# A recurrent attention and a two-layer network on one core: loads moved to GpSimd's queue, and more operands turned by transposing DMAs

## The chip, the cores and the metric

The kernel runs on one core of one Trainium2 chip. The metric is the device time of one execution in microseconds (us). The core has five engines with a queue of instructions each: TensorE (PE, matrix products), VectorE (DVE), ScalarE (ACT), GpSimd (POOL) and SyncE (SP). SP and POOL also issue DMAs, which sixteen DMA engines carry out. Each queue is worked off in order: an instruction that waits holds all that stand behind it.

## The reference

The first part is a gated linear attention over 4 batches, 8 heads, 768 steps and 48 channels per head:

```python
for t in range(S):
    state = alpha[:, :, t, :, None] * state + np.einsum('bhd,bhe->bhde', k[:, :, t], v[:, :, t])
    y[:, :, t] = np.einsum('bhd,bhde->bhe', q[:, :, t], state)
```

The second part takes the 3072 rows of 384 values (all heads of one step side by side) through two matrices:

```python
h = x @ w_in                 # 384 -> 2048
r = np.maximum(h, 0.0)
out = (r * r) @ w_out        # 2048 -> 384
```

## The kernel before

**Chunks.** The 4 x 768 steps are cut into 24 chunks of 128 steps, numbered s = 0 to 23; six chunks are one batch (`c` counts 0 to 5 in it, `last` is c = 5, which needs no state after it). Within a chunk the recurrence is turned into matrix products. With L the logarithm of alpha and P its running sum over the steps of the chunk, q is multiplied by exp(P) and k by exp(-P). The products of these two, cut off above the diagonal, are the scores (`sc`, then `sm`); scores times v, plus scaled q times the state of the chunks before, is the output of the chunk (`py`, copied to `xn`). The state (`st`) adds scaled k times v and is then scaled by exp of the chunk's total.

**Two ways to the scaled q and k.** The scores need q and k with the channels on the partitions, the state product needs k with the steps on them.

- In early chunks (s below `RAW`, 11) the running sum with the steps on the partitions (`e_p0`, one 128x384 product, and four one-column products for the totals) goes through two exponentials (`A`, `Ainv`), DVE makes scaled q and k (`qA_s` L502, `kI_s` L505), and TensorE transposes both (`e_p1q`, `e_p1k`), four products each.
- In later chunks ("raw") POOL casts q and k to bf16 (`rawb`, L413), SP's transposing DMAs turn them (`rawt`, L416), TensorE makes the running sum already turned (`e_pT`, four products), ACT takes its two exponentials (L451 and L454), and DVE multiplies (L507 `e_qAT`, L510 `e_kiT`). Unless the chunk is the last of its batch, `e_p0`, `Ainv` and `kI_s` are still made as before, for the state product alone.

**From attention to the network.** `xn` is turned to `xT_big` by three transposes on TensorE and a copy on DVE; from chunk 18 to 22 (`XTURN`) by one transposing DMA from SP (L620). The first matrix then works in groups of two chunks (products `bank<-xT_big,w_in_b`, relu on ACT L676, square on DVE L684 into `gT`), the second on one chunk at a time (`bank<-w_out_b,gT`, copied to `ob` by ACT or DVE). Outputs leave from SP, those of chunks 5 to 17 that are not held back from POOL (L772).

**Order.** A planner in the kernel (`Plan.run`) gives each step an engine, a reckoned duration, what it depends on and a priority, lists the steps in time with these figures, and emits the instructions in the order of their reckoned starts. The order on each engine is thus fixed before the run: attention steps of chunk s stand between matrix products of chunks some 3.7 earlier (`LEAD`). The planner's classes are PE, ACT, DVE and POOL, "DMA" for loads (first in, first out, 1.0 us each), "TR" for transposing DMAs (1.0 us, landing 4.0 us later) and "OUT"; the last three all go to SP's queue. POOL does casts of v (L405), of raw q and k, and the outputs named above.

**Loads.** Each chunk has four loads of 128 x 8 x 48 fp32 (192 KB, in pieces of 48 values): alpha, q, k and v (`add_load`, L371). All are issued by SP, between its transposes; alpha of chunks 0 to 3 comes as two larger loads. There are six buffers for each of the four.

Of the kernel before, what the change touches and what calls it, by code (L numbers as in the profile page):

```python
# [54 lines left out]
def after(op, x=0.0):  # L55
    return (op, x)
# [85 lines left out]
def kernel(  # L142
# [10 lines left out]
    nc = tc.nc  # L153
# [4 lines left out]
    NP = H // 2  # L158
# [35 lines left out]
        out=utri_f, in_=utri_f, compare_op=ALU.is_ge, fill=0.0,  # L194
# [10 lines left out]
    for c in range(JN):  # L205
        blk = slice(JP * c, JP * c + JP)
        nc.gpsimd.affine_select(
            out=tri4[blk, 0:JW], in_=tri4[blk, 0:JW], compare_op=ALU.is_ge, fill=0.0,
# [27 lines left out]
    def pin(ins):  # L236
        tc.keep_in_program_order(ins)
# [4 lines left out]
    def tr(*a):  # L242
        pin(nc.tensor.transpose(*a))  # L243
# [6 lines left out]
    GLA_BANKS = sl_bank[0:2]  # L250
# [14 lines left out]
    def add(eng, dur, emit, *deps, **kw):  # L265
        return plan.add(Op(eng, dur, emit, deps, **kw))
# [41 lines left out]
    C = [dict() for _ in range(NT)]  # L308
    state = {}
    SRC = dict(srcs)  # L310
    EARLY = 4
    RAW = 11
    XTURN = (18, 23)
    TLD, TLAT, TLATE = 1.0, 4.0, 2.0
    NR = 3
    R = {}

    def raw_tiles():
        if R:
            return  # L320
        R["b"] = stage.tile([P, NR, 2, H, DP], BF16, name="rawb", tag="stage")
        nc.gpsimd.memset(R["b"][:, :, :, :, D:], 0.0)
        R["t"] = stage.tile([P, NR, 2, NP, P], BF16, name="rawt", tag="stage")
        R["i"] = stage.tile([P, 2, NP, P], BF16, name="aiT", tag="stage")

# [38 lines left out]
    def add_load(s, nm):  # L364
        d = C[s]
        b, c = divmod(s, NCH)

        def ld():
            if nm not in d:
                d[nm] = loads.tile([P, H, D], FP32, name=nm)  # L370
            pin(nc.sync.dma_start(out=d[nm], in_=SRC[nm][b, c]))  # L371
        prev = C[s - LB].get("use_" + nm) if s >= LB else None
        d["ld_" + nm] = add("DMA", LD if s < 4 else LD1, ld, prev, lat=2.0 if s < 4 else LAG if s < 6 else 2.4, at=0.6)

    def add_chunk(s):
        d = C[s]
        b, c = divmod(s, NCH)
        i = s % NBUF
        L, qA, kI, ae = L_s[:, i], qA_s[:, i], kI_s[:, i], ae_s[:, i]
        old = C[s - NBUF].get("end") if s >= NBUF else None  # L380
        g = dict(prio=-10.0 + s * 0.01)
        last = c == NCH - 1

        def cast(op, out_t, in_t):
            if op.eng == "ACT":
                pin(nc.scalar.copy(out_t, in_t))  # L386
            elif op.eng == "DVE":
                pin(nc.vector.tensor_copy(out_t, in_t))  # L388
            else:
                pin(nc.gpsimd.tensor_copy(out_t, in_t))  # L390
# [6 lines left out]
        if joint:  # L397
            ln = J["ln"]
        else:
            ln = [add("ACT", 0.41, e_ln, d["ld_at"], old, prio=-15.0 if s < EARLY else -5.0)]  # L400
# [5 lines left out]

        raw = s >= RAW
        if raw:
            w, wz = s % NR, s % 2

            def e_rb(j, nm):
                raw_tiles()
                pin(nc.gpsimd.tensor_copy(R["b"][:, w, j, :, 0:D], d[nm]))  # L413

            def e_turn(j):
                pin(nc.sync.dma_start_transpose(out=R["t"][:, w, j], in_=R["b"][:, w, j].rearrange("p h d -> p (h d)")))  # L416
            rt = []
            for j, nm in enumerate(["qt", "kt"]):
                cb = add("POOL", 0.55, lambda j=j, nm=nm: e_rb(j, nm), d["ld_" + nm],
                         *([C[s - NR]["turn"][j]] if s >= RAW + NR else []), prio=-5.0)  # L420
                d["use_" + nm] = cb
                t_ = add("TR", TLD, lambda j=j: e_turn(j), cb, *([C[s - NR]["turned"][j]] if s >= RAW + NR else []), lat=TLAT)
                t_.late = TLATE
# [17 lines left out]
        p0 = Op("PE", 0.66 if joint else 0.17 if raw else 0.27, e_p0, ln, takes=GLA_BANKS, lat=0.05, **g)  # L441
# [14 lines left out]
        def e_aeT(j):  # L456
            rows = slice(64 * j, 64 * j + 64)
            pin(nc.scalar.activation(ae[rows, :, j], d["pmT"][rows, :, P - 1], AF.Exp))
# [11 lines left out]

        def e_ae1():
            pin(nc.scalar.activation(ae[64:128, :, 1], d["pm"][64:128, HD:HD + NP], AF.Exp))
        if not (raw and last):
            plan.add(p0)
        if not raw:
            a_ = add("ACT", 0.38, e_A, p0, **g)
            ai = add("ACT", 0.38, e_Ai, p0, after(a_), **g)
        if raw:
            ai = None
            if not last:  # L480
                ai = add("ACT", 0.38, e_Ai, p0, **g)
                p0.gives = ai
            pT = Op("PE", 0.23, e_pT, [*ln] + ([] if last else [after(p0)]), takes=GLA_BANKS, **g)
            plan.add(pT)
            if last:
                pT.gla = s
            aT = add("ACT", 0.48, e_AT, pT, after(ai) if ai else None, **g)
            aiT = add("ACT", 0.48, e_AiT, pT, after(aT), *([C[s - 2]["turned"][1]] if s >= RAW + 2 else []), **g)
            pT.gives = aiT
            if not last:  # L490
                ae0 = add("ACT", 0.18, lambda: e_aeT(0), pT, after(aiT), **g)
                pT.gives = ae1 = add("ACT", 0.19, lambda: e_aeT(1), pT, after(ae0), **g)
        elif joint:
            ae1 = J["ae"]
            p0.gives = ai
        else:
            ae0 = add("ACT", 0.18, e_ae0, p0, after(ai), **g)
            ae1 = add("ACT", 0.19, e_ae1, p0, after(ae0), **g)
            p0.gives = ae1
# [8 lines left out]

        def e_kiT():
            pin(nc.vector.tensor_mul(d["qkT"][:, NP:2 * NP, :], R["t"][:, w, 1], R["i"][:, wz]))  # L510
        if raw:
            if not last:
                mk = d["use_kt"] = add("DVE", 0.47, e_kI, ai, d["ld_kt"], old, **g)
            cp = add("DVE", 0.34, e_qAT, aT, rt[0], **g)
            cpk = add("DVE", 0.34, e_kiT, aiT, rt[1], cp, **g)
            d["turned"] = [cp, cpk]
        else:
            mq = d["use_qt"] = add("DVE", 0.47, e_qA, a_, d["ld_qt"], old, **g)
            mk = d["use_kt"] = add("DVE", 0.47, e_kI, ai, d["ld_kt"], old, **g)
# [11 lines left out]
        if not raw:  # L531
            p1q = plan.add(Op("PE", 0.22, e_p1q, [mq], takes=GLA_BANKS, **g))
            p1k = plan.add(Op("PE", 0.22, e_p1k, [mk] if s < EARLY else [mk, after(p1q)], lat=0.15,
                              takes=P1K_BANKS if s < EARLY else None, **g))

        def e_cp(lo, hi):
            if "qkT" not in d:
                d["qkT"] = work.tile([P, 2 * NP, P], BF16, name="qkT")
            cast(cpk if lo else cp, d["qkT"][:, lo:hi, :], d["pTk"][:, 0:NP, :] if lo else d["pT"][:, lo:hi, :])
        if s < EARLY:  # L540
            cp = add({"ACT": 0.49, "DVE": 0.34}, 0, lambda: e_cp(0, NP), p1q, **g)
            cpk = add({"DVE": 0.34, "ACT": 0.49}, 0, lambda: e_cp(NP, 2 * NP), p1k, **g)
# [13 lines left out]
        p2 = d["p2"] = plan.add(Op("PE", 0.42, e_p2, [cp, cpk], takes=[sl_sc], lat=0.10, **g))  # L556
# [9 lines left out]
        if not last:  # L566
# [7 lines left out]
            prev = C[s - 1].get("sb") if s else None  # L574
            if c == 0 and s:
                prev = C[s - 2]["sb"]
# [37 lines left out]
        def e_p4():  # L614
            d["px"] = psum(p4, [P, KT, P], BF16)
            for j in range(KT):
                tr(d["px"][:, j, :], d["xn"][:, j * P:(j + 1) * P], ident_bf)
        if XTURN[0] <= s < XTURN[1]:
            def e_xt():
                pin(nc.sync.dma_start_transpose(out=xT_big[:, :, s * P:(s + 1) * P], in_=d["xn"]))  # L620
# [238 lines left out]
    for op in plan.order:  # L859
        if op.eng == "PE":  # L860
# [3 lines left out]
            if pe_end is not None and DUMMY and not opened and op.start < CALM:  # L864
                n = max(0, int((op.start - pe_end) / 0.11 + (0.4 if op.start < DENSE else -1.8))) + (extra.pop(0) if extra else 0)
# [35 lines left out]
```

## Time and profile before

| | |
|---|---|
| median of 3 runs | 185.1 us (184.77 to 185.87) |
| profiled execution | 185.07 us, of it span 183.4 us |
| instructions | 4946 |
| TensorE: matmuls, busy | 1908, 177.5 us |
| DVE, ACT, POOL busy | 127.1, 126.5, 39.4 us |
| granted clock | 1.00 |
| DMA | 34.12 MB, 80.7% of 16 engines' span on SP's queue, 3.2% on POOL's |

The span is the time from the first to the last instruction of the core; what the whole execution takes beyond it lies around the kernel. In a line of a timeline the columns are start, length in us, engine, source line, operation, destination and sources with their sizes, count, and in brackets the idle time before with what ended it. A line with "<-" in a list of waits reads: this engine, at this line, stood idle for that one, with total, count and longest in us. In the lines of stretches each engine has its busy time and the number of instructions (PE, PEld, DVE, ACT, POOL), then the granted clock, the mean share of the DMA engines that was busy, and GB/s. Matmuls overlap in the records: each shows some 200 to 330 ns, while the next starts earlier.

### The profile page before, as it was taken

To read this page: it belongs to the slowest core of one execution; us is meant where nothing else is said; L and a number is where in the kernel's file an instruction comes from. 1 tells how busy PE (TensorE), PEld (TensorE's weight loads), DVE (VectorE), ACT (ScalarE), POOL (GpSimd) and SP (SyncE) were. 2 spreads that over 40 slices of the span, in tenths; PEclk is the share of its full clock that TensorE was granted. 3 is DMA by queue.
4 is the path that set the end of the run, shared out by engine and by line. 5 is a ranking of instruction groups with operands and counts; after the bars stand their busy time and mean duration, and the time that the engine had idled before them with its cause. 6 is when DMAs were issued, how large, how long until landed. Compare 5 with 4: busy or idle time off the path is not lost.

```text
span 183.4 us, 4946 instructions
## 1 busy us (share of the span) xinstructions
PE 177.5 (97%) x1908; PEld 130.5 (71%) x1908; DVE 127.1 (69%) x273; ACT 126.5 (69%) x286; POOL 39.4 (21%) x80
## 2 busy tenths in 40 slices
PE   7999999899999999999999998999999999999993
PEld 2577884567769877867768776667766777778663
DVE  1179898684999998778877867748855984744200
ACT  3677799226859996966967859847975895767321
POOL 8221100021131142132223133342323512000000
PEclk9999999999999999999999999999999999999999
DMA  5999999999999999998999599898898898901022
GB/s 168 215 212 252 302 366 321 326 220 204 177 191 201 194 179 173 141 190 161 150 193 202 113 240 186 161 227 162 170 201 182 176 163 194 301 13 43 12 77 86
DMA packets 120200, 34.12 MB, mean 186 GB/s; under 512 B 112400, under 2 KB 118928, under 8 KB 120176
## 3 DMA queue, kind: packets, MB, share of 16 engines
q1 hardware_dynamic: 119536, 31.83, 80.7%
q0 software_dynamic: 640, 1.97, 3.2%
q8 instruction: 15, 0.25, 0.6%
q14 instruction: 9, 0.07, 0.2%
HBM read 25.17 MB, written 4.72 MB: 163 GB/s over the span
## 4 chain that ended last, share of the span: by engine, by line
PE 49%; DMA 2%; ACT 1%; issue 0%; DVE 0%
PE bank L240 45%; DMA at<-in_alpha_dram 2%; PE sc L240 2%; PE st L240 1%; PE bank L243 1%; ACT aiT L454 0%; ACT r L676 0%; ACT ob L758 0%; ACT L_s L396 0%; ACT ob L716 0%; DVE xT_big L388 0%; ACT qkT L451 0%
## 5 line engine op out<-in xcount | busy, mean ns | idle before, releaser
L240 PE MATMUL bank<-xT_big,w_in_b 128*128 128x256 bf16 (+2 forms) x636 | 76.6, 262 | 0.9 <-ACT r L676 0.7
L240 PE MATMUL bank<-w_out_b,gT 128*128 128x384 bf16 (+1 forms) x400 | 71.6, 320 | 0.5 <-DVE w_out_b L296 0.5
L676 ACT ACTIVATE r<-bank 128x512 bf16<-128x512 f32 x96 | 56.6, 606 | 11.3 <-PE bank L240 9.9
L240 PEld LDWEIGHTS <-w_in_b 128*128 128x128 bf16 x636 | 52.7, 98 | 10.6 <-issue 1.5
L240 PEld LDWEIGHTS <-gT 128*128 128x128 bf16 x416 | 37.2, 98 | 18.7 <-DVE w_out_b L296 1.0
L684 DVE TENSOR_TENSOR gT<-r 128x512 bf16<-128x512 bf16 x96 | 41.8, 453 | 10.2 <-ACT r L676 9.0
L561 DVE TENSOR_TENSOR sm<-sc,utri_b 128x512 bf16<-128x512 f32 x48 | 30.8, 684 | 5.9 <-PE sc L240 5.7
L405 POOL CAST vb<-vt 128x384 bf16<-128x384 f32 x24 | 13.6, 569 | 69.1 <-DMA vt<-in_v_dram 55.2
L386 ACT CAST xn<-bank 128x384 bf16<-128x384 f32 x24 | 11.6, 482 | 11.6 <-PE bank L240 11.5
L505 DVE TENSOR_TENSOR kI_s<-kt,Ainv 128x384 bf16<-128x384 f32 x21 | 12.8, 611 | 7.8 <-ACT Ainv L466 7.8
L240 PEld LDWEIGHTS <-qkT 64*128 64x128 bf16 (+1 forms) x272 | 10.7, 95 | 6.4 <-issue 2.4
L586 ACT CAST sb<-st 128x384 bf16<-128x384 f32 x20 | 9.6, 482 | 7.7 <-DVE st L581 7.5
L758 ACT COPY ob<-bank 128x384 f32<-128x384 f32 x14 | 6.7, 480 | 8.0 <-PE bank L240 8.0
L396 ACT ACTIVATE L_s<-at 128x384 bf16<-128x384 f32 x20 | 10.5, 527 | 2.4 <-DMA at<-in_alpha_dram 2.3
L240 PE MATMUL bank<-warm 128*128 128x256 bf16 (+1 forms) x54 | 10.9, 348 | 1.3 <-DVE warm L188 1.3
L502 DVE TENSOR_TENSOR qA_s<-qt,A 128x384 bf16<-128x384 f32 x11 | 6.3, 575 | 8.0 <-ACT A L462 8.0
L413 POOL CAST rawb<-qt 128x384 bf16<-128x384 f32 x13 | 7.4, 570 | 20.3 <-DMA qt<-in_q_dram 20.3
L413 POOL CAST rawb<-kt 128x384 bf16<-128x384 f32 x13 | 7.6, 587 | 19.0 <-DMA kt<-in_k_dram 11.1
L581 DVE TENSOR_TENSOR st<-st,ae_s 128x384 f32<-128x384 f32 x20 | 11.1, 556 | 0.5 <-PE st L240 0.5
L466 ACT ACTIVATE Ainv<-bank 128x384 bf16<-128x384 f32 x21 | 10.5, 501 | 1.1 <-PE bank L240 1.0
L240 PE MATMUL sc<-qkT 64*128 64x128 bf16 x192 | 9.5, 219 | 0.0
L240 PEld LDWEIGHTS <-sm 128*128 128x128 bf16 x192 | 8.1, 96 | 1.7 <-issue 0.2
(64 smaller groups left out, 165.7 us busy)
## 6 DMA issues: line engine op xcount, KB each, us to landing
qt<-in_q_dram SPq DMA_DIRECT2D x24, 192.0 KB, 4.0
kt<-in_k_dram SPq DMA_DIRECT2D x24, 192.0 KB, 3.6
vt<-in_v_dram SPq DMA_DIRECT2D x24, 192.0 KB, 3.8
at<-in_alpha_dram SPq DMA_DIRECT2D x20, 192.0 KB, 4.0
wo<-in_moe_w_out_dram SPq DMA_DIRECT2D x4, 768.0 KB, 8.5
out_dram<-ob POOLq DMA_DIRECT2D x10, 192.0 KB, 3.1
wi<-in_moe_w_in_dram SPq DMA_DIRECT2D x4, 384.0 KB, 5.3
wi<-in_moe_w_in_dram SPq DMA_DIRECT2D x2, 768.0 KB, 8.3
```

Source lines behind the costliest of these rows:

```text
L240: pin(nc.tensor.matmul(*a, **kw))
L386: pin(nc.scalar.copy(out_t, in_t))
L396: pin(nc.scalar.activation(L[:, :, 0:D], d["at"], AF.Ln))
L405: pin(nc.gpsimd.tensor_copy(d["vb"], d["vt"]))
L413: pin(nc.gpsimd.tensor_copy(R["b"][:, w, j, :, 0:D], d[nm]))
L466: pin(nc.scalar.activation(d["Ai"], d["pm"][:, 0:HD].rearrange("p (h d) -> p h d", h=H), AF.Exp, scale=-1.0))
L505: pin(nc.vector.tensor_mul(kI[:, :, 0:D], d["kt"], d["Ai"]))
L561: pin(nc.vector.tensor_mul(d["sm"][:, hh], d["sc"][:, hh], utri_b.to_broadcast([P, NP, P])))
L581: pin(nc.vector.tensor_mul(st4, st4, bcast(ae, D)))
L586: pin(nc.scalar.copy(d["sbt"], d["st"]))
L676: pin(nc.scalar.activation(box["r"][:, 0:w], box["ph"][:, 0:w], AF.Relu))
L684: pin(nc.vector.tensor_mul(gT[g][:, f0:f0 + per, lo * P:lo * P + n], r, r))
```

## The change

Four things change:

- Loads of chunk 12 and later (`PL`) are issued by POOL. In the planner such a load is a step of POOL of 0.9 us that lands 5.0 us later (`PL_LAT`) and may not start before the scores of the chunk three earlier (`PL_AHEAD`); this condition only orders the steps, the instruction itself waits for its buffer.
- `RAW` is 10 in place of 11: chunk 10 takes the later way to its scaled q and k.
- `XTURN` begins with chunk 16 in place of 18: x of chunks 16 and 17 is turned by DMA too.
- From chunk 18 on (`KTURN`), unless the chunk is the last of its batch (18 to 22), `e_p0`, `Ainv` and the DVE product for `kI_s` are left out. Scaled k, which DVE has already made with the channels on the partitions for the scores, is turned back into `kI_s` by a transposing DMA from SP (`e_kn`), and the state product waits for that.

Together there are 48 loads from POOL in place of SP, and nine transposing DMAs more (two for chunk 10, two of x, five of keys). The core of the diff:

```diff
-    RAW = 11
-    XTURN = (18, 23)
+    RAW = 10
+    PL, PL_AHEAD, PL_LAT = 12, 3, 5.0
+    XTURN = (16, 23)
...
+    KTURN = 18
...
-            pin(nc.sync.dma_start(out=d[nm], in_=SRC[nm][b, c]))
+            pin((nc.gpsimd if s >= PL else nc.sync).dma_start(out=d[nm], in_=SRC[nm][b, c]))
         prev = C[s - LB].get("use_" + nm) if s >= LB else None
+        if s >= PL:
+            o = d["ld_" + nm] = add("POOL", 0.9, ld, prev, C[s - PL_AHEAD]["p2"], prio=4.0, lat=PL_LAT)
+            o.moves = 0.85
+            return
...
+        kd = s >= KTURN and not last
+        nat = not (s >= RAW and (last or kd))
...
-        if not (raw and last):
+        if nat:
             plan.add(p0)
...
-            if not last:
+            if nat:
                 ai = add("ACT", 0.38, e_Ai, p0, **g)
                 p0.gives = ai
...
+        def e_kn():
+            pin(nc.sync.dma_start_transpose(out=kI.rearrange("p (n a) d -> p n (a d)", a=2),
+                                            in_=d["qkT"][:, NP:2 * NP, :].rearrange("p n t -> p (n t)")))
         if raw:
-            if not last:
+            if nat:
                 mk = d["use_kt"] = add("DVE", 0.47, e_kI, ai, d["ld_kt"], old, **g)
             cp = add("DVE", 0.34, e_qAT, aT, rt[0], **g)
             cpk = add("DVE", 0.34, e_kiT, aiT, rt[1], cp, **g)
             d["turned"] = [cp, cpk]
+            if kd:
+                mk = add("TR", 0.65, e_kn, cpk, old, lat=TLAT)
+                mk.late = 0.5
```

More of the change, by code (lines that the diff above doesn't have):

```diff
@@ L479, in add_chunk @@
             ai = None
-            if not last:
+            if nat:
                 ai = add("ACT", 0.38, e_Ai, p0, **g)
                 p0.gives = ai
-            pT = Op("PE", 0.23, e_pT, [*ln] + ([] if last else [after(p0)]), takes=GLA_BANKS, **g)
+            pT = Op("PE", 0.23, e_pT, [*ln] + ([after(p0)] if nat else []), takes=GLA_BANKS, **g)
             plan.add(pT)
-            if last:
+            if not nat:
                 pT.gla = s
```

## The prediction

> **What bounds the kernel now.** I read the busy shares first, then the stretches of the middle of the run, then TensorE's own timeline, and last what the few gaps wait for. TensorE is busy for 97% of the span, no other engine for more than 71%.
>
> ```profile
> PE 177.5 (97%) x1908; PEld 130.5 (71%) x1908; DVE 127.1 (69%) x273; ACT 126.5 (69%) x286; POOL 39.4 (21%) x80
> ...
> rawt<-rawb SPq DMA_TRANSPOSE x26, 3.4
> ```
>
> In stretches of 20 us from 60 to 160 us, which is where the change acts, TensorE idles 0.75 of 100 us at full clock. DVE and ACT each have 23 us to spare, POOL 71. The DMA engines do not: their shares add up to 93 of 100 us.
>
> ```profile
> 60.00:80.00 20.00, 20.00 (x244) 16.19 (x241) 18.31 (x39) 16.60 (x39) 5.48 (x10) 1.00 0.96 174
> 80.00:100.00 20.00, 19.92 (x210) 14.79 (x209) 15.54 (x34) 14.98 (x35) 5.90 (x11) 1.00 1.00 176
> 100.00:120.00 20.00, 19.33 (x197) 14.24 (x196) 14.48 (x34) 15.84 (x37) 5.80 (x11) 1.00 0.90 180
> 120.00:140.00 20.00, 20.00 (x202) 14.09 (x199) 13.44 (x28) 14.52 (x35) 7.28 (x14) 1.00 0.91 189
> 140.00:160.00 20.00, 20.00 (x212) 15.18 (x211) 14.52 (x30) 14.75 (x34) 4.38 (x8) 1.00 0.88 200
> ```
>
> So a matrix instruction less is time less, as long as nothing new makes TensorE wait. Matmuls overlap in the records, so their price is the distance from one start to the next. The timeline of TensorE has the pairs:
>
> ```profile
> 66.38 0.24 PE L240 MATMUL bank<-ones_t,L_s 128*128 128x1 bf16 x4
> 66.48 0.36 PE L240 MATMUL bank<-vb,sm 128*128 128x48 bf16 x8
> ...
> 68.31 0.33 PE L243 MATMUL bank<-ident_bf,xn 128*128 128x128 bf16 x3
> 68.48 1.46 PE L240 MATMUL bank<-w_out_b,gT 128*128 128x384 bf16 x8
> ...
> 69.83 0.38 PE L243 MATMUL bank<-ident_bf,qA_s 128*128 128x128 bf16 x4
> 70.05 0.49 PE L240 MATMUL bank<-xT_big,w_in_b 128*128 128x256 bf16 x3
> ...
> 73.34 0.39 PE L240 MATMUL bank<-utri_b,L_s 128*128 128x128 bf16 x4
> 73.56 0.49 PE L240 MATMUL bank<-xT_big,w_in_b 128*128 128x256 bf16 x3
> ...
> 128.17 0.33 PE L240 MATMUL bank<-L_s,utri_b 128*128 128x384 bf16 x1
> 128.33 0.49 PE L240 MATMUL bank<-xT_big,w_in_b 128*128 128x256 bf16 x3
> ```
>
> The one gap of the middle is 0.66 us before 111.84. The chain of waits leads it back to an alpha load on SP's queue, and the list of waits names it:
>
> ```profile
> 105.28 4.13 DMA at<-in_alpha_dram
> 109.42 0.34 ACT L_s L396
> ...
> 110.70 0.60 ACT aiT L454
> ```
>
> ```profile
> PE bank L240 <- ACT r L676: 0.7, 1, 0.7
> ```
>
> ACT stood 0.71 us behind a logarithm whose load was late, and the relu behind it kept TensorE. On SP that load stood behind a transpose that held the queue for 3.48 us.
>
> **The change, part by part.** As built, the changed program has 19 matmuls less. *Cumulative sum of chunks 18 to 22* (128x384, the line at 128.17): 5 x 0.16 = 0.80 us off. *Transposes of x of chunks 16 and 17* (68.31 to 68.48): 2 x 0.17 = 0.34 off. *Chunk 10 turned by DMA*: q and k lose four transposes each (0.22 + 0.22) and the four one-column products (0.10), and it gains four transposed sums (73.34 to 73.56, 0.22): 0.32 off. Together 1.46 us off the engine that sets the end.
>
> What goes with it on DVE and ACT (five Ainv at 0.50 us, five kI at 0.61, two x copies at 0.35, chunk 10's exponentials and products swapped) I cost at nothing: the matrix work covers it, with 23 us of idle on each engine in these 100 us. The same cover holds for what chunk 10 adds to ACT, and its two casts more on POOL (0.57 us each) fall where POOL idles.
>
> *The gap of 0.66 us.* The alpha loads no longer stand behind transposes. The bounds are 0 (the load is late again on POOL) and 0.66; I take 0.66 off, since the row that made it is the queue that the loads leave. What is late next are the keys for the state.
>
> *Forty-eight loads on POOL*, four a chunk from chunk 12 on. POOL works in order, so casts and loads queue behind one another, and behind a late load stand ACT's logarithm (the gap above again) and the transposes on SP. The trace has no load issued by POOL. The nearest rows are the 128x384 outputs, on both queues:
>
> ```profile
> L772 POOL DMA_DIRECT2D out_dram<-ob x10: 539/539/692, 97.1 to 152.9; - x10
> L772 SPq DMA_DIRECT2D out_dram<-ob x5: 332/332/350, 159.2 to 178.4; - x5
> ```
>
> An output row is one piece of 1536 B, a load has eight pieces of 192 B per row. The floor for a load is thus 0.54 us (pieces cost nothing), the ceiling 8 x 0.54 = 4.3 us (only pieces cost). On SP the same two forms stand at 0.33 and about 0.55 us (0.53 to 0.57 for loads that nothing holds), a ratio of 1.65, so I take 0.54 x 1.65 = 0.9 us. A chunk takes 6.8 us now (sc at 77.30 for chunk 11, 158.61 for chunk 23), and 6.7 us after. POOL's other work in it is three casts (0.57, 0.57, 0.59) and an output in most chunks (0.45 on average): 2.18 us. With 4 x 0.9 that is 5.8 of 6.7 us, so POOL keeps up, and I cost it at nothing. The cover is thin: it is gone at (6.7 - 2.18) / 4 = 1.13 us a load. It needs a second thing: a cast of q waits for a load that was issued right behind the chunk before's cast, so issue to landing must stay under some 6 us. Loads from SP land after 3.6 to 4.0 us (median), outputs from POOL after 3.1.
>
> *SP's queue* loses these loads (0.53 to 0.57 us each, over 2 us a chunk) and gains nine transposes of about 1.2 us; with two for q and k, one for x and one for the keys it is busy 4.8 of 6.7 us. It is also in order: a q transpose that waits for POOL's cast holds the key transposes behind it.
>
> *The DMA engines.* The 93 us are ten outputs (3.2% of 183.4 = 5.9 us) and some 55 loads and 31 transposes, about 1.0 us each. Nine transposes more make 102 of 100 us. Shares over 1.00 occur (1.07 from 20 to 30 us), so 100 is no hard end, and part of it moves to other places; I cost it at nothing, with 0 and 2 us as bounds.
>
> *Keys for the state, chunks 18 to 22.* The product kI was ready before the scores; now it lands by DMA after them. In the changed order 4.2 (chunk 20) to 4.9 us (chunk 22) of matrix work stands between the first score and the state product, priced with the rows above (0.11 us per 256 columns, 0.165 per 384). The q and k transposes land 3.4 us after issue (median; 2.5 to 5.9), and one more transpose ahead on SP adds 1.2. So the wait of each is between 0 and 1.7 us, of all five between 0 and 8.5; a gain is excluded, as TensorE never waits for kI there now. I take 0.3 us, one or two of the five slightly late, since the median row fits with about 1 us to spare.
>
> **Sum.** The profiled execution took 185.07 us, 183.4 of it span, and the median is 185.1, so one base serves both: 185.07 - 0.80 - 0.34 - 0.32 - 0.66 + 0.3 = 183.25, predicted as 183.3.
>
> **Rivals.** *POOL's issue is the new bound (the other side).* For it: software must write eight times the pieces of any DMA that POOL issues now. Against it: SP's ratio of 1.65. It decides above 1.13 us a load. At 1.3 us the queue falls back 0.68 us a chunk over 11 chunks, 7.5 us, less the 1.4 us by which loads are issued early (5.9 us reserved, 4.5 expected): 185.07 - 1.46 + 6.1 = 189.7. At 1.5 us it is 198.5.
>
> *POOL is shut out while DVE runs bf16 products.* A cast beside such a product took 0.77 instead of 0.51 us, but an output beside one (DVE's L507 from 137.84) took the usual 0.54:
>
> ```profile
> 133.60 0.77 POOL L413 CAST rawb<-kt 128x384 bf16<-128x384 f32 x1 [0.92 <-DMA kt<-in_k_dram]
> ...
> 137.60 0.54 POOL L772 DMA_DIRECT2D out_dram<-ob  x1 [1.30 <-ACT ob L758]
> ```
>
> DVE does four gT products (0.45), L507 (0.46) and L510 (0.44) a chunk, 2.7 of 6.7 us. Were 40% of the 3.6 us of issue stretched by as much again, POOL would need 7.2 us a chunk: 0.53 x 11 - 1.4 = 4.4 us lost, 188.0. The Trainium skill, page "SBUF — State Buffer", section "SBUF: two separate sides", speaks against the change here: descriptors for a DMA issued from GpSimd cannot be written while DVE holds the shared port, and it advises the other queues. The cast's row agrees with it, the output's row does not.
>
> *The DMA engines are full.* If 102 us do not fit in 100, the 2 us come back: 185.07 - 1.46 + 2 = 185.6, more if landings pass 6 us. For it speaks the 0.93 share, against it that TensorE's list of waits names no DMA now. The Trainium skill's page "DMA: Bandwidth & Descriptors", section "Issuing engines are not separate DMA queues", says that a second issuing engine saves only the issue time; no row here can show it yet.
>
> *The key transposes are late each time*, by 0.5 us: 185.07 - 1.46 - 0.66 + 2.5 = 185.5, about the time before.
>
> **How the numbers follow.** About 0.5% (0.93 us) is what a measurement of this kernel tells from no change. The forecast gets 0.56, all of it faster. Late keys 0.10 (0.02 faster, 0.06 same, 0.02 slower), full DMA engines 0.12 (half same, half slower), POOL's issue 0.15 (slower), the shut-out 0.07 (0.01 same, 0.06 slower). That is 0.58 faster, 0.13 same, 0.29 slower. The forecast's own range is 182.6 (no key late, a little less at the edges) to 184.0 (the gap stays, keys 0.5 late in all). The whole range goes down to 182.4 and up to 190.0: it takes in the shut-out, the full engines and POOL's issue up to 1.3 us, and leaves out what lies above, with half of that rival.
>
> **What would show it.** Right: 1889 matmuls with TensorE's busy time down by some 1.5 to 2 us, POOL's load issues at 0.8 to 1.1 us with idle time left, no gap at ACT's logarithm, state products waiting for kI_s by less than 0.5 us in all. Wrong: load issues above 1.13 us and POOL without idle time, gaps of TensorE behind relu whose chain leads to a load; landings over 6 us; or waits of st for kI_s of 0.5 us and more each.

## The result: 4.8% slower, and the profile after

The changed kernel takes 194.08 us (median; 192.41 to 197.31) against 184.99 us (184.03 to 187.01) for the kernel before on the same chip: a ratio of 1.048, with a 95% interval of 1.043 to 1.052. The forecast was 183.3 us and a range up to 190.0; both are missed. The profiled execution took 193.22 us, 191.4 of it span. Some executions of most kernels take over 1.5% longer than the fastest of the same kernel; the ratios here leave these out, the medians and ranges of times do not, and one experiment had too few others for a ratio.

The busy shares of the page, after the change:

```profile
PE 177.4 (93%) x1888; PEld 129.7 (68%) x1889; DVE 124.0 (65%) x267; ACT 124.9 (65%) x281; POOL 79.3 (41%) x130
```

The 19 matmuls are gone (1889 weight loads, 1908 before; one matmul record is missing). TensorE is busy as long as before and the span is 8.0 us longer. Where it idles, the stretches of 20 us tell (columns as before: busy time of PE, PEld, DVE, ACT, POOL, then clock, DMA share, GB/s):

```profile
60.00:80.00 20.00, 19.89 (x229) 15.80 (x226) 18.79 (x41) 16.32 (x37) 14.19 (x21) 1.00 0.99 163
80.00:100.00 20.00, 19.15 (x200) 14.22 (x199) 13.84 (x31) 15.21 (x36) 14.93 (x22) 1.00 1.16 189
100.00:120.00 20.00, 20.00 (x213) 14.87 (x211) 16.08 (x34) 15.90 (x37) 15.79 (x24) 1.00 1.05 183
120.00:140.00 20.00, 17.37 (x172) 12.23 (x171) 9.14 (x20) 12.08 (x29) 18.54 (x29) 1.00 1.08 206
140.00:160.00 20.00, 16.63 (x156) 11.43 (x154) 10.97 (x25) 10.76 (x25) 4.76 (x8) 0.91 0.78 134
```

From 60 to 160 us TensorE idles 6.96 us (before: 0.75), 6.0 us of it after 120 us, where the key transposes begin. The rest of the 8.0 us is 0.9 us of idle time in the first 20 us, which the change does not touch, and 0.9 us more between the last matmul and the end. POOL is nearly full from 120 to 140 us (18.54 of 20). The gaps stand in TensorE's timeline with what ended them:

```profile
85.19 0.36 PE L240 MATMUL bank<-vb,sm 128*128 128x48 bf16 x8 [0.59 <-POOL vb L413]
...
131.27 0.34 PE L240 MATMUL st<-vb,kI_s 128*128 128x96 bf16 x4 [1.72 <-DMA kI_s<-qkT]
...
132.95 0.40 PE L240 MATMUL sc<-qkT 64*128 64x128 bf16 x8 [0.68 <-DVE qkT L518]
...
141.36 0.40 PE L240 MATMUL sc<-qkT 64*128 64x128 bf16 x8 [0.87 <-DVE qkT L518]
...
148.26 0.50 PE L240 MATMUL st<-vb,kI_s 128*128 128x96 bf16 x4 [2.51 <-DMA kI_s<-qkT]
```

The first gap, of 0.59 us, stands behind POOL's cast of v, which had itself waited 1.4 us for a load of v. After 120 us two state products wait for their transposed keys (4.2 us together), and two groups of scores wait for scaled k (1.6 us). The list of waits has one row further back:

```profile
DVE qkT L518 <- DMA rawt<-rawb: 3.6, 2, 3.1
```

So the scores are late because the q and k transposes are. None of these waits stands in the list of before. The rows of DMA queues and issues (queue: packets, MB, share of 16 engines' span; issue: count, median us to landing) show how much later loads and transposes land:

```profile
q1 hardware_dynamic: 74256, 23.50, 56.7%
q0 software_dynamic: 3712, 11.41, 31.4%
...
qt<-in_q_dram POOLq DMA_DIRECT2D x12, 192.0 KB, 6.1
...
rawt<-rawb SPq DMA_TRANSPOSE x28, 5.5
...
xT_big<-xn SPq DMA_TRANSPOSE x7, 5.1
kI_s<-qkT SPq DMA_TRANSPOSE x5, 4.8
```

Before, `rawt` landed after 3.4 us, `xT_big` after 2.5 and the loads from SP after 3.6 to 4.0. The chain of waits joins the pieces (start, length, what):

```profile
126.30 7.05 DMA kt<-in_k_dram
...
133.46 0.60 POOL rawb L421
...
135.56 5.20 DMA rawt<-rawb
...
140.88 0.43 DVE qkT L518
...
141.37 6.85 DMA kI_s<-qkT
148.21 0.05 issue
148.26 0.50 PE st L240 x4
```

A load of k from POOL lands after 7.05 us, its cast is late, the transpose of it takes 5.20 us, and the keys made from that come back after 6.85 us. SP's timeline shows a second cause, the order of its queue:

```profile
122.49 1.18 SPq L634 DMA_TRANSPOSE xT_big<-xn  x1
124.36 1.22 SPq L520 DMA_TRANSPOSE kI_s<-qkT  x1
125.67 1.27 SPq L424 DMA_TRANSPOSE rawt<-rawb  x1
127.90 1.97 SPq L634 DMA_TRANSPOSE xT_big<-xn  x1
132.95 1.19 SPq L520 DMA_TRANSPOSE kI_s<-qkT  x1
```

The `rawt` of 125.67 is k of chunk 19. POOL had cast it by 121.4, but in front of it on SP stood x of chunk 17, which waited for ACT, and the keys of chunk 18, which waited for DVE's product. It left 4.3 us late, took 6.7 us to land and gave the gap at 132.95. The k transpose behind the gap at 141.36 left 1.5 us after its cast, behind the keys of chunk 19 and its own q.

The gap before 148.26 has an aftermath. In stretches of 2 us (the last three columns are clock, DMA share and GB/s):

```profile
148.00:150.00 2.00, 1.74 (x9) 1.06 (x10) 1.20 (x3) 0.48 (x1) 0.00 (x0) 0.50 0.98 242
150.00:152.00 2.00, 2.00 (x19) 1.31 (x17) 0.03 (x1) 0.60 (x1) 0.00 (x0) 0.71 0.32 66
152.00:154.00 2.00, 2.00 (x27) 1.79 (x27) 1.96 (x4) 1.50 (x3) 0.00 (x0) 1.00 0.00 0
```

The granted clock is 0.50, then 0.71. From 148.26 to 151.56 TensorE did four state products, four 128x384 and nine 128x256 products, which at the prices of the prediction and 0.18 us for the four state products (145.75 to 145.93 before) make 1.83 us; they took 3.30. In this execution these 1.47 us eat up the whole saving of matrix work.

### The profile page after: what moved, and what is told of

Same layout as the page of the kernel before. It is cut to its first block, busy times and chain, and to the rows that moved or that the text cites. A ratio compares the mean times of both kernels' runs of the same rounds, so it can differ in the third digit from the quotient of the medians.

```text
span 191.4 us, 4901 instructions
## 1 busy us (share of the span) xinstructions
PE 177.4 (93%) x1888; PEld 129.7 (68%) x1889; DVE 124.0 (65%) x267; ACT 124.9 (65%) x281; POOL 79.3 (41%) x130
## 3 DMA queue, kind: packets, MB, share of 16 engines
q0 software_dynamic: 3712, 11.41, 31.4%
## 4 chain that ended last, share of the span: by engine, by line
PE 56%; DMA 23%; ACT 7%; DVE 6%; POOL 3%; issue 2%; SPq 0%; DVEq 0%; POOLq 0%; ACTq 0%
PE bank L240 50%; DMA kt<-in_k_dram 6%; DMA wi<-in_moe_w_in_dram 5%; DMA kI_s<-qkT 4%; DMA vt<-in_v_dram 3%; DMA rawt<-rawb 3%; PE sc L240 3%; PE bank L243 3%; ACT r L690 2%; DMA at<-in_alpha_dram 2%; DMA qt<-in_q_dram 1%; DVE gT L698 1%; PE st L240 1%; POOL rawb L421 1%; DVE qkT L518 1%
## 5 line engine op out<-in xcount | busy, mean ns | idle before, releaser
L240 PE MATMUL bank<-w_out_b,gT 128*128 128x384 bf16 (+1 forms) x400 | 70.5, 322 | 0.5 <-DVE w_out_b L296 0.5
L690 ACT ACTIVATE r<-bank 128x512 bf16<-128x512 f32 x96 | 56.0, 605 | 7.9 <-PE bank L240 6.6
L413 POOL CAST vb<-vt 128x384 bf16<-128x384 f32 x24 | 13.1, 548 | 54.3 <-DMA vt<-in_v_dram 44.2
L772 ACT COPY ob<-bank 128x384 f32<-128x384 f32 x12 | 5.8, 480 | 16.4 <-PE bank L240 16.4
L513 DVE TENSOR_TENSOR kI_s<-kt,Ainv 128x384 bf16<-128x384 f32 x16 | 10.3, 645 | 3.0 <-ACT Ainv L474 3.0
L786 POOL DMA_DIRECT2D out_dram<-ob x10 | 5.6, 560 | 14.7 <-DVE ob L770 10.5
L515 DVE TENSOR_TENSOR qkT<-rawt,qkT 128x512 bf16<-128x512 bf16 x14 | 6.2, 445 | 7.4 <-ACT qkT L459 6.1
L240 PE MATMUL bank<-warm 128*128 128x256 bf16 (+1 forms) x54 | 9.8, 319 | 1.3 <-DVE warm L188 1.3
L373 POOL DMA_DIRECT2D at<-in_alpha_dram x12 | 10.8, 902 | 0.0
L240 PE MATMUL st<-vb,kI_s 128*128 128x96 bf16 x80 | 6.9, 210 | 4.2 <-DMA kI_s<-qkT 4.2
```

Source lines behind the costliest of these rows:

```text
L240: pin(nc.tensor.matmul(*a, **kw))
L373: pin((nc.gpsimd if s >= PL else nc.sync).dma_start(out=d[nm], in_=SRC[nm][b, c]))
L413: pin(nc.gpsimd.tensor_copy(d["vb"], d["vt"]))
L513: pin(nc.vector.tensor_mul(kI[:, :, 0:D], d["kt"], d["Ai"]))
L690: pin(nc.scalar.activation(box["r"][:, 0:w], box["ph"][:, 0:w], AF.Relu))
```

## The experiments

Three explanations compete: POOL, with its casts behind 48 issues, is too full to be in time; the DMAs land later because there is a second queue, or more to move; the transposes are held up by the order and the waits of SP's queue. Every time is compared with the kernel before, on the same chip; the edits are shown against the changed kernel unless another one is named.

### The change taken apart

**Loads alone.**

```diff
-    RAW = 10
+    RAW = 11
...
-    XTURN = (16, 23)
+    XTURN = (18, 23)
...
-    KTURN = 18
+    KTURN = 24
```

> Only the loads from chunk 12 on move to POOL; no transposing DMA more, so 1908 matmuls as before. Theory F (the DMA engines are full: nine more transposes ask for 102 us of 100): the DMA work is that of before, 93 of 100 us, so transposes land after some 3.5 to 4.2 us as before and the time is that of before less at most the 0.66 us of the alpha gap, 184.3 to 185.5. Theory Q (loads on a second queue slow SP's transposes, whatever the amount): rawt lands at 5 us or more in the median and the time is 187 or more. Theory K (only the keys' way by DMA harms): as before, 184.3 to 185.5.

Measured: 186.04 us, ratio 1.011 (1.008 to 1.014). The bytes and the transposes are those of before, the loads' queue alone differs, and yet the issue row of `rawt` reads:

```profile
rawt<-rawb SPq DMA_TRANSPOSE x26, 4.9
```

TensorE idles 1.37 us between 60 and 160 us, 0.68 of it before a group that waits for `xT_big`. The loads cost something by themselves, but only a quarter of the loss. None of the expected ranges holds: the landing is close to theory Q's 5 us, the time is below its 187.

**Everything but the loads on POOL.**

```diff
-    PL, PL_AHEAD, PL_LAT = 12, 3, 5.0
+    PL, PL_AHEAD, PL_LAT = 24, 3, 5.0
```

> The whole change, but all loads stay on SP. Theory F: the nine transposes are there, so the engines are asked for the same 102 us; landings above 5 us, st waits for kI_s by several us, 189 or more. Theory Q: one queue only, transposes land after about 3.5 us, 1.46 us less matrix work, 183.3 to 184.3. Theory K: 189 or more, the waits all at st for kI_s.

Measured: 190.02 us, ratio 1.036 (1.029 to 1.043). Here `rawt` lands after 3.3 us, and POOL is idle for 70 of the 100 us from 60 to 160, so neither longer landings of q and k nor a full POOL can be the reason of this part. The waits that the changed kernel has are there nonetheless:

```profile
PE sc L240 <- DVE qkT L518: 2.8, 2, 2.3
PE st L240 <- DMA kI_s<-qkT: 1.2, 1, 1.2
```

Three quarters of the loss are there without POOL's loads: all loads and nine transposes more then share SP's queue. Theories F and K had 189 or more, but F expected landings above 5 us and K waits at the state products alone; neither came.

**Everything but the key transposes.**

```diff
-    KTURN = 18
+    KTURN = 24
```

> The whole change without the keys' transposes (chunks 18 to 22 make kI_s on DVE again). Matrix work 0.66 us less than before (0.34 + 0.32). Theory F: 97 of 100 us asked, landings between (4 to 5 us), time 184 to 187. Theory Q: loads on POOL still there, rawt lands at 5 us or more, products of q and k late for the scores, 187 or more. Theory K: nothing left that harms, 183.5 to 184.5.

Measured: 184.96 us, ratio 1.006 (1.001 to 1.010), just above theory K's 184.5. In the middle it has one gap of over 0.3 us, 1.21 us for `xT_big`. The stretch in which its POOL is fullest:

```profile
120.00:140.00 20.00, 20.00 (x208) 14.31 (x207) 12.83 (x27) 14.53 (x36) 18.15 (x28) 1.00 1.10 206
```

POOL has 18.15 of 20 us, the DMA share is 1.10, `rawt` lands after 4.9 us, and TensorE does not idle at all. A POOL that full and landings that late do little harm as long as no key comes back through SP. Adding the key transposes turns 0.6% into 4.8%.

**The key transposes alone.**

```diff
-    RAW = 10
-    PL, PL_AHEAD, PL_LAT = 12, 3, 5.0
-    XTURN = (16, 23)
+    RAW = 11
+    PL, PL_AHEAD, PL_LAT = 24, 3, 5.0
+    XTURN = (18, 23)
```

> Only the keys' transposes of chunks 18 to 22; loads on SP, RAW 11, XTURN from 18. Matrix work 0.80 us less than before. Theory F: 98 of 100 us asked, landings 4 to 5 us, 185 to 188. Theory Q: 184 to 185. Theory K: 188 or more, st waiting for kI_s by 4 us or more in all.

Measured: 185.75 us, ratio 1.011 (1.007 to 1.016). Two gaps:

```profile
150.64 0.40 PE L240 MATMUL sc<-qkT 64*128 64x128 bf16 x8 [0.91 <-DVE qkT L518]
156.58 0.34 PE L240 MATMUL st<-vb,kI_s 128*128 128x96 bf16 x4 [1.26 <-DMA kI_s<-qkT]
```

By themselves the keys already cost more than the 0.80 us of sums that they save, and both kinds of gap are here, with keys that land after 3.3 us (median). Theory K's 188 us did not come. The parts do not add up: loads alone 1.1, keys alone 1.1, chunk 10 and x alone 1.2 (below), together 4.8%.

**Chunk 10 and x of chunks 16 and 17 alone.**

```diff
-    PL, PL_AHEAD, PL_LAT = 12, 3, 5.0
+    PL, PL_AHEAD, PL_LAT = 24, 3, 5.0
...
-    KTURN = 18
+    KTURN = 24
```

> Only chunk 10 turned by DMA and x of chunks 16 and 17; loads stay on SP, no key transposes. Matrix work 0.66 us less than before. Theory F: 97 of 100 us asked of the DMA engines, but one queue alone, landings about 3.5 us, 183 to 184.5 on a chip where before takes 184.1 to 185.1. Theories P and C: 183 to 184.5 too. If it is slower than before, SP's queue in order is what is full.

Measured: 186.59 us, ratio 1.012 (1.006 to 1.018). It saves 0.66 us of products and is slower, against all three theories: four transposes more on an SP that still has all the loads, and TensorE idles 2.2 us between 60 and 160 us. With the loads on POOL as well, the change without the key transposes has 1.006.

### Is POOL too full?

**Long pieces.** The loads from POOL read one run of 192 KB, 1536 B per row, in place of eight pieces of 192 B. The values are then those of other steps; the work is the same.

```diff
+    FLAT = {n: a.rearrange("b h s d -> (b h s d)").rearrange("(n p f) -> n p f", p=P, f=HD)
+            for n, a in [("at", alpha), ("qt", q), ("kt", k), ("vt", v)]}
...
-            pin((nc.gpsimd if s >= PL else nc.sync).dma_start(out=d[nm], in_=SRC[nm][b, c]))
+            if s >= PL:
+                pin(nc.gpsimd.dma_start(out=d[nm].rearrange("p h d -> p (h d)"), in_=FLAT[nm][s]))
+                return
+            pin(nc.sync.dma_start(out=d[nm], in_=SRC[nm][b, c]))
```

> The whole change, but each load that POOL issues reads one run of 192 KB from the same array (1536 B per row in place of eight pieces of 192 B; the values are those of other steps, so what is computed from chunk 12 on is not the reference). Bytes, order and waits are the same. Theory F (the DMA engines' time for small pieces is what is short): the landings of SP's transposes fall from 5 to 7 us back to 3.5 us or less, st hardly waits for kI_s, 182.5 to 184.3 us. Theory P (POOL itself is too full, 18.5 of 20 us from 120 to 140 us): fast as well, since a load with few pieces should take POOL 0.55 us and not 0.88. Theory C (the way of the keys is too long by itself for the 4.2 to 4.9 us that the order leaves): still 188 or more.

Measured: 190.05 us, ratio 1.028 (1.021 to 1.034). An issue on POOL falls from 0.88 to 0.55 us, `rawt` lands after 4.6 us, `kI_s` after 3.5. The state products wait 0.7 us (4.2 before this edit), the scores 4.2 us (1.6). The loss shrinks to 2.8%; of the three expectations theory C's 188 or more holds. This takes both POOL's time and part of the DMA time away, so it needed the next one.

**Long pieces, POOL kept busy.** On top of the long pieces, a memset after each load takes POOL's time up again.

```diff
+    idle = consts.tile([P, 288], BF16)
...
                 pin(nc.gpsimd.dma_start(out=d[nm].rearrange("p h d -> p (h d)"), in_=FLAT[nm][s]))
+                pin(nc.gpsimd.memset(idle, 0.0))
```

> As the run with long pieces, and after each such load POOL clears a small tile that nobody reads (about 0.3 us), so that POOL is as full as in the change. Theory F: as fast as with long pieces alone, 182.5 to 184.5. Theory P: the loss is back, 188 or more. Theory C: 188 or more.

Measured: 189.39 us, ratio 1.023 (1.015 to 1.032), no worse than without the memset. POOL's rows (busy time, mean ns of one):

```profile
L378 POOL MEMSET idle<- 128x288 bf16 x48 | 17.1, 357 | 0.0
...
L377 POOL DMA_DIRECT2D qt<-in_q_dram x12 | 6.6, 547 | 0.0
```

0.357 + 0.547 = 0.90 us a load, against 0.88 in the changed kernel. So what the long pieces gained did not come from POOL's time, and without the key transposes a POOL just as full cost little (above). A full POOL falls as the explanation.

### The order on SP and the place of the state product

**The state product later.** The planner is told that a key transpose lands 3.0 us later; the state products then stand further behind the scores.

```diff
-                mk = add("TR", 0.65, e_kn, cpk, old, lat=TLAT)
+                mk = add("TR", 0.65, e_kn, cpk, old, lat=TLAT + 3.0)
```

> The whole change; the planner is told that a key transpose lands 3.0 us later, so the state product stands 7.3 to 7.6 us of matrix work behind the first score in place of 4.2 to 4.9. Theory F: the waits of st for kI_s go (4.2 us in the profile of the change), those for late q and k transposes stay or grow, 186 to 190. Theory P: nothing gained, 191 or more. Theory C: 183.5 to 186.

Measured: 189.3 us, ratio 1.024 (1.016 to 1.032). This is within theory F's 186 to 190. No state product waits any more. One gap of over 0.3 us is left, of the other kind:

```profile
131.66 0.40 PE L240 MATMUL sc<-qkT 64*128 64x128 bf16 x8 [2.62 <-DVE qkT L518]
```

**q and k first.** The planner places transposes by the reckoned start plus an allowance; these two numbers put the q and k transposes ahead of keys and x.

```diff
-    TLD, TLAT, TLATE = 1.0, 4.0, 2.0
+    TLD, TLAT, TLATE = 1.0, 4.0, 0.0
...
-                mk.late = 0.5
+                mk.late = 1.0
```

> The whole change; on SP the q and k transposes of the next chunk stand ahead of the key transposes and of x (two planner delays changed: 2.0 to 0.0 for q and k, 0.5 to 1.0 for the keys). Same DMAs, same matmuls, same order on the other engines. In the change the k transpose of chunk 19 stood in SP's queue from 121.4 (cast done) to 125.67 behind x of chunk 17 and the keys of chunk 18. Theory S (SP's order: transposes that are ready wait behind ones that wait for ACT and DVE): the waits of the scores for L518 go (1.6 us on TensorE, 2.8 on its weight loads), the keys of chunk 18 land as late as before; 189 to 192. If S is all of it, 184 to 186. Theory F (both queues ask more of the DMA engines than they give): transposes still land after 5 to 7 us, 191 to 195.

Measured: 188.15 us, ratio 1.022 (1.017 to 1.027). Now the waits of the scores are gone and those of the state are left:

```profile
130.60 0.34 PE L240 MATMUL st<-vb,kI_s 128*128 128x96 bf16 x4 [1.01 <-DMA kI_s<-qkT]
...
137.21 0.34 PE L240 MATMUL st<-vb,kI_s 128*128 128x96 bf16 x4 [0.98 <-DMA kI_s<-qkT]
...
144.59 0.34 PE L240 MATMUL st<-vb,kI_s 128*128 128x96 bf16 x4 [0.43 <-DMA kI_s<-qkT]
```

The order on SP alone is worth 2.6 of the 4.8%: shown, since nothing else is changed and `rawt` still lands after 5.2 us. It is more than theory S expected (189 to 192). Of the 5.1 us between the two profiled executions, 3.6 are idle time of TensorE from 60 to 160 us, mostly the scores' 1.6 and 1.8 less at the state. Both edits work, each on its own kind of gap, so I put them together.

**Both.** The two edits above in one kernel.

> The two together: q and k transposes first on SP, and the state product 3.0 us later in the order. Theory S with the thin cover of the keys: nothing waits for kI_s or L518 by more than some tenths, and the 1.46 us less of matrix work show, 183 to 185.5. Theory F: landings of 5 to 7 us keep q and k late all the same, 187 or more.

Measured: 193.6 us (188.81 to 196.34), too scattered for a ratio. None of the four executions comes near the expected 183 to 185.5, so the two gains did not add up. In the profiled one (196.34 us) `kI_s` lands after 10.0 us (median); why is open.

**q and k first, without the key transposes.** The change with `KTURN = 24` and `TLATE = 0.0`.

> The change without the key transposes, q and k transposes ahead of x on SP. Without this order the same kernel was 0.6% slower than before, with 1.2 us of wait for x and late transposes. Theory S: 183.5 to 184.6. Theory F: no better than without, 184.6 to 186.

Measured: 186.25 us, ratio 1.011 (1.005 to 1.016). Without keys in the queue the new order gains nothing (1.006 without it), and theory S's 184.6 or less is missed.

**q and k first, long pieces.** The edits of the two runs of these names together (the loads' values again those of other steps).

> The two mends that each took part of the loss, together: POOL's loads in one run of 192 KB (values of other steps, so the output is not the reference from chunk 12 on), and q and k transposes ahead of the keys and of x on SP. If SP's order and the time in flight of transposes beside POOL's loads are all of it, nothing above some tenths is left on TensorE: 183 to 185 where before takes 184.4. If a third cause is there, 186 or more, and its wait shows in the list of TensorE.

Measured: 186.01 us, ratio 1.009 (1.006 to 1.012). `kI_s` lands after 2.5 us (5.7 with the new order alone) and the only wait for it is this:

```profile
PE st L240 <- DMA kI_s<-qkT: 0.2, 1, 0.2
```

The order on SP and what the long pieces take away, which the run with the busy POOL leaves as the landings, together account for 3.9 of the 4.8%. With the waits gone the kernel still does not beat the one before, though it has 1.46 us less to multiply; its profiled execution (184.88 us) idles 1.09 us between 60 and 160 us. This remainder is open.

**Key transposes alone, q and k first.** The edits of the run with the key transposes alone and of the one with q and k first.

> Only the key transposes of chunks 18 to 22 (0.80 us less matrix work), loads on SP, q and k transposes ahead of the keys on SP. With SP's order as planned before, it was 1.1% slower than before, landings 3.3 us. If the order is what cost there: 183.3 to 184.4, st waiting for kI_s under 0.5 us. If loads and transposes on one queue in order cost as much in another place: 185 or more.

Measured: 188.57 us (185.56 to 189.11); the ratio, 1.014 (1.004 to 1.024), rests on two of the four executions and is not to be told from the 1.011 that the keys alone have without the new order. Where all loads stay on SP, no gain of the order is shown. In the profiled execution (189.11 us) the scores no longer wait, but three state products do, 3.1 us together.

**The same, the state product 1.5 us later.**

```diff
-                mk = add("TR", 0.65, e_kn, cpk, old, lat=TLAT)
+                mk = add("TR", 0.65, e_kn, cpk, old, lat=TLAT + 1.5)
```

> The same, and the planner is told that a key transpose lands 1.5 us later. If the cover of the keys was too short even at landings of 3.3 us: 183.2 to 184.2, below the run without it. If not: the same as that run.

Measured: 186.67 us, ratio 1.013 (1.007 to 1.019); the state waits 0.5 us, and one group waits 1.0 us for `xT_big`. The state's waits are shorter than in the run before, but the time is not to be told from it, as the second expectation had it.

### Which loads cost what

Open was why the loads alone cost 1.1% with the same bytes.

**Alpha alone on POOL** (12 loads). The edit stands on that of the loads alone, here and in the next one.

```diff
-            pin((nc.gpsimd if s >= PL else nc.sync).dma_start(out=d[nm], in_=SRC[nm][b, c]))
+            pin((nc.gpsimd if s >= PL and nm in ("at",) else nc.sync).dma_start(out=d[nm], in_=SRC[nm][b, c]))
-        if s >= PL:
+        if s >= PL and nm in ("at",):
```

> The kernel before with only the alpha loads of chunk 12 and later on POOL (12 of the 48). If each load beside SP's queue lengthens the transposes' landing by its share, rawt lands after 3.4 + 12/48 x 1.5 = 3.8 us (median) and the time is a quarter of the 1.1% that all 48 cost, 0.3% above before, less up to 0.66 us (0.35%) where ACT's gap behind the alpha load goes: ratio 0.997 to 1.003. If it is not the share but any load on a second queue that does it, rawt lands after 4.5 us or more and the ratio stays at 1.008 or above.

Measured: 186.09 us against 185.88, ratio 0.999 (0.995 to 1.003); `rawt` lands after 4.0 us. Both are as the expectation by share has them.

**Alpha and v** (24 loads; `("at", "vt")` in the same lines).

> The kernel before with the alpha and v loads of chunk 12 and later on POOL (24 of the 48); q and k stay on SP. By share: rawt lands after 3.4 + 0.5 x 1.5 = 4.1 us, ratio 1.002 to 1.006. If the loss of all 48 comes from the q and k loads, which stand on POOL in the same queue as the casts that the transposes wait for, this kernel is like the one with alpha alone: ratio within 0.003 of it, whatever the landing.

Measured: 185.24 us against 185.88 for the kernel before, ratio 0.995 (0.991 to 1.000). The expectation by share of loads (1.002 to 1.006) is missed. In the profiled execution (187.59 us) `rawt` lands after 5.3 us, no sooner than with all 48 loads (4.9). Half the loads on POOL cost nothing that shows, and the interval touches no change; the 1.1% came with the other half, the q and k loads, as the second expectation had it, to within the intervals. No run has q and k alone on POOL, so that it is these loads and not their number, and that they act through the casts behind them in POOL's queue, is argued, not shown.

**Alpha and v on POOL, chunk 10 and x by DMA, no key transposes.** The edit of the run before, on the change without the key transposes.

> The change without the key transposes, and with the q and k loads back on SP (24 loads on POOL, alpha and v). If the q and k loads on POOL are what the loads cost, this beats the 1.0057 of the change without the key transposes: ratio 0.993 to 1.002, less matrix work and no load in front of a cast. If SP's queue cannot hold q and k loads beside four more transposes, as when all loads stay on SP (1.0117), the ratio is 1.006 or more with waits for xn, xT_big or qkT.

Measured: 185.69 us against 185.28, ratio 1.002 (0.999 to 1.006): no difference, with one gap of 0.31 us in the middle. It meets neither expectation fully: above the 1.002 of the one only by the interval's width, and without the waits of the other.

**Alpha and v on POOL, the whole change, q and k first.** The same edit on the change with q and k first.

> The whole change with q and k transposes ahead of keys and x on SP, and the q and k loads back on SP. With all 48 loads on POOL this order gave 1.0218. If the loss that is left comes from the q and k loads on POOL, the ratio is 1.000 to 1.010 and the state products wait less than 1 us in all; if it comes from the way of the keys through SP, which these loads fill more, it is 1.02 or above with waits of 2 us and more for kI_s.

Measured: 189.98 us against 185.28, ratio 1.025 (1.019 to 1.031), as with all loads on POOL (1.022). Moving the q and k loads back to SP thus does not cure what is left after the order is mended; the expectation of 1.000 to 1.010 is missed, and that of 1.02 or more fits, with one wait of 2.71 us for `kI_s` in the profile. Whether these loads cost as much on SP as they did on POOL, by another way, the run can't tell. The key transposes, with the new order, make the difference again: 1.002 without the two, 1.025 with them. Of all these kernels only alpha and v on POOL may be faster than before, by 0.5% with an interval that reaches no change.

## Why the prediction was wrong, step by step

**Matrix products, 1.46 us off: right, but not seen.** The 19 products are gone. In the profiled execution the clock that fell after one gap took 1.47 us back. The prediction has no term for the clock.

**Gap at ACT's logarithm, 0.66 us off: not gained.** That gap is gone, but alpha is late again, once: issued by POOL at 77.50, it lands 7.3 us later and ACT waits 2.0 us for it (0.71 before). At the same time TensorE idles the 0.59 us before 85.19, behind POOL's cast of v, which the prediction did not name among what stands behind a late load.

**POOL's issue at 0.9 us, costed at nothing: right.** The changed kernel's rows of this line (ns: least, median, most) say 0.88 us between bounds of 0.54 and 4.3, under the limit of 1.13 (the longest of all 48 issues, the first, took 1.05):

```profile
L373 POOL DMA_DIRECT2D qt<-in_q_dram x12: 882/882/894, 67.7 to 138.4; - x12
L373 POOL DMA_DIRECT2D kt<-in_k_dram x12: 882/882/891, 69.0 to 139.9; - x12
```

The rival that POOL's issue is the bound falls with it. The ratio of SP's two forms (1.65) carried over to POOL (0.88 to 0.55, 1.6).

**POOL shut out while DVE runs bf16 products: fell.** Issues that ran beside DVE's product for `gT` from start to end (72.99, 101.50, 115.16) took 0.88 to 0.89 us, and those beside no DVE instruction (79.78, 107.40, 121.33) took 0.88. The rule of the Trainium skill (page "SBUF — State Buffer", section "SBUF: two separate sides"), that DVE's hold on the shared port keeps GpSimd from writing descriptors, is given there for DVE operations in a 2-port mode, and for two inputs in SBUF only against a GpSimd operation that reads SBUF. The prediction carried it over to issues beside products of two inputs, and there these rows show no wait.

**Landings under 6 us: not held.** The medians of POOL's loads are 5.4 to 5.7 us and, for q, 6.1; single loads took more (7.05 in the chain), as the text's own list of what would show it wrong had it.

**The DMA engines, 0 to 2 us, costed at nothing: mis-sized, with the wrong mechanism.** The text counted busy time (93 and 9 more) and asked whether it fits. The DMA share from 60 to 160 us is 1.01, and loads alone on POOL have 0.90 and still lengthen `rawt` from 3.4 to 4.9 us. Landing time was the quantity to forecast, not the share. Where a transfer's landing has slack (the change without the key transposes, alpha and v alone on POOL) that costs little; where landings follow each other, as the load of k, its transpose and then its keys, each lengthens the chain. The Trainium skill (page "DMA: Bandwidth & Descriptors", section "Issuing engines are not separate DMA queues") says that DMAs from different issuing engines interleave on the same 16 DMA engines and that a second issuer saves only issue time. The runs agree that it gains no more; beyond it they show the 1.5 us by which the other queue's transposes landed later.

**SP's queue, "busy 4.8 of 6.7 us", costed at nothing: the step that failed first.** The text had a late q transpose holding key transposes behind it. It did not look at the other direction: a key or x transpose that waits for DVE or ACT holds q and k transposes that are ready (4.3 and 1.5 us before the two gaps at the scores). Busy time leaves that wait out. Putting q and k first took 2.6 of the 4.8% back.

**Keys for the state, 0.3 us: the step that failed most.** They cost 4.2 us at the state, and through SP 1.6 us at the scores. The cover of 4.2 to 4.9 us was about right, but the landing was taken from the trace of before (3.4), where neither POOL's loads nor the nine transposes stood beside it. In the changed kernel keys land after 4.8 us (median); the two that were waited for left SP as soon as DVE had made them (124.36 and 141.37) and took 6.9 us each. The total of 4.2 lies inside the text's 0 to 8.5, so the choice of 0.3 was the error, but its bound of 1.7 us a wait was passed (1.72 and 2.51). That bound is 5.9 - 4.2 and leaves out the 1.2 us of a transpose ahead that the text had just named: with it the bound is 2.9, and the median (3.4 + 1.2) leaves hardly anything to spare. The waits of the scores were not in its sum. Its rival of late keys had the place, but priced each at 0.5 us and forgot that the scores' inputs stand behind the keys on SP.

**The chances.** No rival held the outcome. (The forecast's upper edge of 184.0 is 184.1 by its own terms, 183.25 + 0.66 + 0.2; nothing hangs on it.) The one on the slower side that was priced above 189 put the loss on POOL's issue; most of the loss came through SP, from its order, which had been costed at nothing, and from landings that had been taken from the kernel before.

## What to carry to other kernels

Before moving work from an engine to a DMA, ask for each queue what stands behind the new instruction while it waits, not only how long it is busy; a transpose that waits for a late product holds every ready one behind it. Price a landing by the traffic that will be there after the change, and count it once for each link of a chain that goes through the same queue twice. A small saving on the busiest engine (here 1.46 us) can be gone with a single gap after which its clock is lower.

## What the runs showed of the hardware

- **Pieces and POOL's issue.** 1024 pieces of 192 B take POOL 0.88 us, 128 pieces of 1536 B 0.55 us, hence some 0.4 ns of POOL for each of the 896 pieces more. POOL's queue counts 64 packets a load either way (3712 - 640 = 3072 more for 48 loads). SP's queue loses 1040 packets with each load that leaves it (119,536 before, 69,616 with the loads alone on POOL).
- **A second queue lengthens the first one's landings.** With equal bytes, the median landing of `rawt` went from 3.4 us to 4.0 (12 loads moved), 5.3 (24) and 4.9 (48). Over all profiles it is 3.3 to 3.6 us in the six kernels with every load on SP, and 4.0 to 5.7 in the fourteen with loads on POOL. Why is open; long pieces shortened it only from 5.5 to 4.6 in the whole change.
- **The clock.** A gap of 2.51 us was followed by a granted clock of 0.50 and 0.71 over the next 4 us. The clock also fell, to 0.50 to 0.52 in a stretch of 2 us, after gaps of 2.62 us (state product later), 2.71 (alpha and v on POOL, q and k first) and 2.04 (key transposes alone, q and k first). It stayed at 1.00 after 2.05 and 2.17 us (long pieces), 2.31 (everything but the loads on POOL) and 2.40 (POOL kept busy). The length of the gap alone thus does not decide it. The Trainium skill (page "TensorE: Matmul & The Clock Gate", section "HAM oscillation — how this bites in real kernels") gives gaps above about 3.4 us as those to avoid; here 2.0 to 2.7 us were enough four times.
